# Two layers of attention and GLU on one core: a table of step orders for even and odd units, and the stages of the last tiles set apart

## The chip, the core and the metric

The kernel runs on one core of a Trainium2 chip. The core has TensorE (PE; its weight loads are listed apart as PEld), VectorE (DVE), ScalarE (ACT), GpSimd (POOL) and SyncE (SP), each with its own in-order instruction stream. SP issues nearly all transfers, POOL a few. The metric is device time in microseconds (us); lower is better.

## The reference

The input x is 2048 x 448. Attention, GLU, attention, GLU are applied with the same weights in both layers, each on a layer-normalised input and added to x. Attention has 16 heads of 28 for the queries, and one shared head of 28 for keys and values:

```python
q = (x @ wq).reshape(B, S, H, Dh).transpose(0, 2, 1, 3)
k = x @ wk
v = x @ wv
p = softmax(einsum("bhqd,bkd->bhqk", q, k) * Dh ** -0.5)
x = x + einsum("bhqk,bkd->bhqd", p, v)[heads side by side] @ wo
g, u = x_n @ w_gate, x_n @ w_up        # x_n: layer norm of x; 448 -> 1792
x = x + (sigmoid(g) * u) @ w_down
```

## The kernel before, in words

**Numbers.** Products run on pairs of half-precision tensors, a high and a low part. So a product of depth 448 is a chain of 11 matmuls (`chain`, L345), and the down product takes 3 matmuls for each of its 14 slices of 128 (L784).

**Units and steps.** Each layer has 16 units `u` of 128 queries, and each unit 16 steps `kt` of 128 keys, so 256 steps to a layer. A step has three kinds of attention work on PE:

- `S` (`scores`, L581): one matmul `s` (L584) for four heads; ACT takes its exponential into a tile `P` (L587). A step has four.
- `P` (`pv`, L590): the four matmuls `pv` (L595) of a finished step's `P` with the values. The trace shows each as two records, so one step is "x8" and two steps are "x16". These steps stand in a list `waiting`.
- `M` (a step of `Maxima`, L489): four matmuls `mx` (L549) into four PSUM banks and four DVE reductions `mp` (L554), for the row maxima of a later unit. A finished row of maxima is transposed (`mt`, L575), copied (`mr`, L577) and stored by POOL into row 28 of that unit's query tile `QS` (L578). Its place is set by a count of visits (`late`, L579).

`F` is a slice of filler (`Filler.slice`, L864): matmuls of any generator that has work, up to a budget of estimated ns. Fillers are the GLU of a block of two tiles (`bulk`, L732: `gp`, `up`, `dn`), the query projections `qp` (`qgen`, L425) and the output products `wo` (L685, three to a slice, ahead of the others). `X` is a tick (L610): each chain of stages in `side` counts down and runs its next stage when its count is zero. It also sets the budget of the following slices, from the filler that is left over the steps that are left. Operations put off by `defer` (L66) run a given number of slices later.

**Order.** PE takes its instructions in the order in which the program writes them. For the first units (u below 4 in layer 0, below 3 in layer 1) a string of letters gives one step (`ORDER`, `LATER`, L1037 and L1041); for all others `PAIR` (L1042) gives a step of even and a step of odd `kt`. In `PAIR` both `P` of a pair stand together in the even step.

**PSUM.** `s`, `mx` and every filler's accumulator share one tag `f` of seven banks; `pv` has the eighth.

**Stages of a tile** (`Block.tile`, L631). After a unit ends, 11 stages bring its rows to the block's input: the sums go out to memory and back (`f0` L639, `fx` L647), are inverted (`fy`), stored (`fz` L657), read back broadcast (`fw` L664, tile `lb`), multiplied on POOL (`fa` L669), split on ACT and DVE (`fb`, tile `oT`), then the products `wo` (`fc`), layer norm (`fd`), a transposing transfer on SP (`fe`, L340, tile XT2) and the start of the block's GLU (`ff`). The number before each stage is the ticks that it waits.

**Keys of the next layer** (L788 to L843). After a tile's `dn` its layer norm (`db`), transpose (`dc` by a transfer on SP, or `dct` on PE for the last block), product `kv` (`dd`), the transpose of the keys (`de`, `det`) and the count (`df`) follow, again by ticks.

**The tails.** After step 255 of a layer a loop (L1121) ticks and fills until the next layer's first unit has its maxima, or, in layer 1, until nothing is left. The list `fine` becomes non-empty when the last tile's `dn` is done, and the loop then uses other slices.

**Query tiles.** `load_qs` (L438) brings the next unit's `QS` (two buffers) by 12 transfers on SP (L445).

## Time and profile before

| what | us |
|---|---|
| three runs: median (lowest to highest) | 2290.93 (2286.94 to 2293.14) |
| the profiled execution: its own time | 2284.06 |
| its span, first to last instruction | 2282.3 |
| PE busy | 2213.4 (97%) |
| DVE busy | 1638.6 (72%) |
| ACT busy | 1545.7 (68%) |
| POOL busy | 338.1 (15%) |

The profiled execution is 6.9 us below the median of the three runs. A row of the timeline reads: start, duration, engine, line, operation, what it writes and reads, sizes, count; in brackets the idle time of the engine before it, and what ended that. [...]

### The profile page before, as it was taken

What the parts mean: (1) busy time and instruction counts of PE and PEld (TensorE: products, weight loads), DVE (VectorE), ACT (ScalarE), POOL (GpSimd) and SP (SyncE); (2) the same over time, 40 slices, a digit from 0 to 9 for tenths busy, and PEclk for the clock granted to TensorE, in tenths of its full rate; (3) what the DMA queues carried; (4) which work ended last, traced back from release to release, by engine and by line L of the source; (5) the groups of instructions that cost most, each with busy time, mean ns of one, the idle gap of its engine ahead of it and who ended that gap; (6) DMA issues with size and microseconds to landing.
All of it is one profiled execution on the core that took longest, in us unless ns stands there. A gap on an engine that the chain in (4) does not pass through costs nothing.

```text
span 2282.3 us, 41511 instructions
## 1 busy us (share of the span) xinstructions
PE 2213.4 (97%) x15915; PEld 1030.0 (45%) x15915; DVE 1638.6 (72%) x2905; ACT 1545.7 (68%) x2595; POOL 338.1 (15%) x590
## 2 busy tenths in 40 slices
PE   8998999999999999999999999999999999999989
PEld 3322353444545444454563224444444545444456
DVE  7988887777777777777795547777777777777322
ACT  5797786666667677676514997767676767667731
POOL 5114781001110110001011111000000000000010
PEclk9999999999999999999999999999999999999999
DMA  4333661323313142332341123233232313232233
GB/s 144 101 109 97 206 220 45 107 71 97 113 51 113 41 121 65 97 104 75 107 134 39 31 60 103 73 90 94 84 88 65 99 42 116 63 92 86 77 108 111
DMA packets 203623, 213.29 MB, mean 93 GB/s; under 512 B 135376, under 2 KB 164240, under 8 KB 203424
## 3 DMA queue, kind: packets, MB, share of 16 engines
q1 hardware_dynamic: 198080, 195.78, 29.5%
q0 software_dynamic: 5344, 14.87, 1.8%
q8 instruction: 124, 2.03, 0.4%
q14 instruction: 75, 0.61, 0.1%
HBM read 175.37 MB, written 23.59 MB: 87 GB/s over the span
## 4 chain that ended last, share of the span: by engine, by line
PE 59%; DVE 6%; ACT 3%; DMA 1%; issue 1%; SPq 0%; POOL 0%; ACTq 0%; DVEq 0%; POOLq 0%
PE pv L595 14%; PE s L584 13%; PE dn L784 9%; PE up L352 8%; PE gp L352 7%; PE mx L549 4%; DVE mp L554 4%; PE wo L695 2%; ACT P L587 2%; PE qp L352 1%; ACT h L757 0%; DVE th L754 0%; DMA rc<-sums 0%; DVE h L758 0%; DMA XT<-hl 0%
## 5 line engine op out<-in xcount | busy, mean ns | idle before, releaser
L587 ACT ACTIVATE P<-s,esc 128x512 f32<-128x512 f32 x2048 | 1291.4, 689 | 477.1 <-PE s L584 462.1
L554 DVE TENSOR_REDUCE mp<-mx 128x1 f32<-128x512 f32 x2048 | 1269.1, 682 | 398.6 <-PE mx L549 395.7
L584 PE MATMUL s<-QS,KK 96*128 96x512 f16 x2048 | 699.3, 380 | 29.7 <-DVE mp L554 12.0
L352 PEld LDWEIGHTS <-wgu 128*128 128x128 f16 x4928 | 456.3, 97 | 231.3 <-issue 89.8
L595 PE MATMUL pv<-P,VV 128*32 128x512 f32 x4096 | 506.0, 602 | 0.6 <-ACT pvs L599 0.6
L352 PE MATMUL gp<-XT,wgu 128*128 128x256 f16 x2464 | 364.7, 273 | 0.7 <-ACT P L587 0.6
L352 PE MATMUL up<-XT,wgu 128*128 128x256 f16 x2464 | 362.4, 273 | 0.8 <-DVE mp L554 0.4
L784 PE MATMUL dn<-WD,h 128*128 128x448 f16 x1344 | 314.4, 353 | 0.0
L584 PEld LDWEIGHTS <-KK 96*128 96x128 f16 x2048 | 198.1, 98 | 142.6 <-issue 44.3
L595 PEld LDWEIGHTS pv<-P,VV 128*32 128x32 f32 x4096 | 101.3, 109 | 263.6 <-issue 259.9
L549 PE MATMUL mx<-KK,QH 32*128 32x512 f16 x1792 | 188.4, 385 | 3.3 <-DVE mp L554 2.2
L784 PEld LDWEIGHTS <-h 128*128 128x128 f16 x1344 | 122.3, 97 | 139.4 <-issue 30.6
L549 PEld LDWEIGHTS <-QH 32*128 32x128 f16 x1792 | 46.1, 91 | 256.3 <-issue 253.2
L669 POOL TENSOR_TENSOR lb<-pvs,lb 128x512 f32<-128x512 f32 x32 | 40.9, 1278 | 627.3 <-DMA lb<-sums 446.1
L757 ACT ACTIVATE h<-th 128x512 f16<-128x512 f32 x112 | 70.5, 630 | 88.5 <-DVE th L754 88.5
L352 PE MATMUL qp<-XT,WQ 128*128 128x512 f16 x352 | 115.4, 387 | 1.0 <-DVE mp L554 0.4
L306 POOL TENSOR_SCALAR rs<-mv 128x1 f32<-128x1 f32 (+1 forms) x50 | 12.1, 242 | 693.5 <-DVE mv L291 647.7
L746 ACT ACTIVATE th<-gp,gsc 128x512 f32<-128x512 f32 x112 | 77.1, 688 | 40.7 <-PE gp L352 40.4
L754 DVE SCALAR_TENSOR_TENSOR th<-th,up 128x512 f32<-128x512 f32 x112 | 75.8, 677 | 35.3 <-PE up L352 34.7
L695 PE MATMUL wo<-WO,oT 128*128 128x448 f16 x384 | 94.5, 358 | 6.5 <-ACT oT L675 6.1
L758 DVE SCALAR_TENSOR_TENSOR h<-th,h 128x512 f16<-128x512 f32 x112 | 77.9, 696 | 31.3 <-ACT h L757 30.7
L352 PEld LDWEIGHTS <-WQ 128*128 128x128 f16 x352 | 33.2, 98 | 62.5 <-issue 37.7
(151 smaller groups left out, 915.9 us busy)
## 6 DMA issues: line engine op xcount, KB each, us to landing
wgu<-wgu_d SPq DMA_DIRECT2D x224, 512.0 KB
QS<-qd SPq DMA_DIRECT2D x384, 32.0 KB
lb<-sums SPq DMA_DIRECT2D x128, 64.0 KB
xr<-in_A_x_dram SPq DMA_DIRECT2D x32, 224.0 KB
qd<-qst POOLq DMA_DIRECT2D x28, 256.0 KB, 2.7
wgu_d<-sgu POOLq DMA_DIRECT2D x14, 512.0 KB, 4.2
x2d<-x SPq DMA_DIRECT2D x16, 224.0 KB
xr<-x2d SPq DMA_DIRECT2D x16, 224.0 KB
```

Of the source, the lines that this page charges most:

```text
L352: nc.tensor.matmul(ps, a, b, start=n == 0, stop=n == 10)
L549: nc.tensor.matmul(ps[h][:, i * w:(i + 1) * w], qh[32 * h:32 * h + 32, g], KK[l][32 * h:32 * h + 32, 1, ka:kz], start=True, stop=True, til ...
L554: nc.vector.tensor_reduce(o, ps[h].rearrange("p (g k) -> p g k", g=n), axis=AX.X, op=OP.max)
L584: nc.tensor.matmul(s, KK[l][0:96, 0, kt * 128:(kt + 1) * 128], QS[l, u][:, g].rearrange("p h n -> p (h n)"), start=True, stop=True)
L587: nc.scalar.activation(p, s, AF.Exp, scale=esc)
L595: nc.tensor.matmul(v[32 * g:32 * g + 32], VV[l][:, kt], P[g], start=kt == 0, stop=kt == KT - 1, tile_position=(0, 32 * g))
L695: nc.tensor.matmul(p, v["oT"][:, a, h * 128:(h + 1) * 128], WO[:, c, h], start=n == 0, stop=n == 11)
L746: defer(lambda: nc.scalar.activation(th, gp.rearrange("p j n -> p (j n)"), AF.Tanh, scale=gsc))
L754: nc.vector.scalar_tensor_tensor(t, th, 1.0, up.rearrange("p j n -> p (j n)"), op0=OP.add, op1=OP.mult)
L757: nc.scalar.activation(h[:, 0], t, AF.Copy, scale=2.0 ** -17)
L758: defer(lambda: nc.vector.scalar_tensor_tensor(h[:, 1], t, 2.0 ** -17, h[:, 0], op0=OP.mult, op1=OP.subtract), 1)
L784: nc.tensor.matmul(p, hs[f // 2][:, a, o:o + 128], WD[:, f, c], start=n == 0, stop=n == 3 * FC - 1)
```

## The change

Six things change; the numbers of instructions on PE stay the same.

1. `PATHS` holds a pair of orders for each stretch: A for the first four units of layer 0 (as before), B0 and B1 for its later even and odd units, C for the first three units of layer 1, D0 and D1 for its later even and odd units. Where both steps of a pair have a `P`, each `P` does all that waits, else one step.
2. The next unit's `QS` is loaded at `kt` 9 and no longer at 5. In D1 the odd step holds two `M`, so that the load, which stands in the branch of `M`, is written twice there. The second goes to the same buffer.
3. In the tails a tick has three slices of 600 and no longer four of 450. Once `fine` holds the last tile, a tick has four slices of 450 and no longer two.
4. The keys' stages: the transfer `dc` one tick after `db`, `kv` four ticks later; `dct` and `det` of the last block's first tile one tick later each.
5. GLU: the split of `h` on ACT three slices after `th` (two before), its low part on DVE two slices later (one before).
6. Layer 1's units 0 to 2: `fd` one tick later. `Maxima` of the next layer is made two steps later, a row of maxima for units 1 to 3 is stored one visit earlier, and layer 1 starts with half a query product of filler (three quarters before).

```diff
-        late.append([2 if l and u in AHEAD else LT, fin, (l, u)])
+        late.append([1 if l and u in AHEAD else LT, fin, (l, u)])
...
-            return ..., (3 + (l and u < 3), fd), (3, fe), (2, ff)
+            return ..., (3 + 2 * (l and u < 3), fd), (3, fe), (2, ff)
...
-                                                                     op1=OP.subtract), 1)
-                    defer(parts, 2)
+                                                                     op1=OP.subtract), 2)
+                    defer(parts, 3)
...
-                    later((2, db), (2, dct), (1, dd), (1, det), (1, df))
+                    later((2, db), (3, dct), (1, dd), (2, det), (1, df))
                 else:
-                    later((2, db), (3, dc), (2, dd), (2, de), (2, df))
+                    later((2, db), (1, dc), (4, dd), (2, de), (1, df))
...
-    ORDER = "FSFSFSFSPXM"
-    LATER = "FSFSFSPFSXM"
-    PAIR = ("FSFSXFSSPPM", "FSSFSXFSFM")
-    HEAD = U * KT - 32
+    HEAD = U * KT - 30
+    PATHS = {
+        "A": ("FSFSFSFSPXM", "FSFSFSFSPXM"),
+        "B0": ("SFSFSXSPPM", "SSXFFSFFSMF"),
+        "B1": ("FFSSXFFSSPMP", "SSFSFXSFM"),
+        "C": ("FXFFSSSSPPM", "SFFFSSSFXMFF"),
+        "D0": ("FSFSFXFSSPPM", "SSFFXSFSFM"),
+        "D1": ("FSFSXFSSPP", "MSFSSFXFFSM"),
+    }
...
-        fill.slice((0.75 if l else 0.4) * QCH)
+        fill.slice((0.50 if l else 0.4) * QCH)
...
-                    if kt == 5 and u + 1 < U:
+                    if kt == 9 and u + 1 < U:
                         load_qs(l, u + 1)
...
-                    for _ in range(len(waiting) if not paired else min(1, len(waiting))):
+                    for _ in range(len(waiting) if single else min(1, len(waiting))):
                         pv(*waiting.pop(0))
...
-            for _ in range(0 if fine else 4):
-                fill.slice(VS / 4)
+            for _ in range(0 if fine else 3):
+                fill.slice(VS / 3)
...
-            for _ in range(2 if fine else 0):
+            for _ in range(4 if fine else 0):
                 fill.slice(VS / 4)
```

How the instructions move is shown at three places.

**SP, the end of layer 1**: the stages of the last tile (`rc` is fx, `sums` fz, `lb` fw, the transpose into XT fe) among the loads of GLU weights (`wgu`) and the stores of the result. Before:

```order
L639 DMA sums_107<-pvs 4x512
L641 DMA xr<-x2d 128x448
L647 DMA rc<-sums_107 128x16
L657 DMA sums_107<-rc 128x16
L730 DMA wgu<-wgu_d 128x2048 x2
L664 DMA lb<-sums_107 32x512 x4
L730 DMA wgu<-wgu_d 128x2048 x2
L340 DMA_TRANSPOSE XT_28238<-hl 128x7x128
L796 DMA out_dram<-x_28506 128x448
```

With the change:

```order
L639 DMA sums_107<-pvs 4x512
L641 DMA xr<-x2d 128x448
L647 DMA rc<-sums_107 128x16
L730 DMA wgu<-wgu_d 128x2048 x2
L657 DMA sums_107<-rc 128x16
L664 DMA lb<-sums_107 32x512 x4
L730 DMA wgu<-wgu_d 128x2048 x2
L796 DMA out_dram<-x_28583 128x448
L340 DMA_TRANSPOSE XT_28316<-hl 128x7x128
```

A pair of weight loads has moved ahead of the store of the inverted sums, and a store of the result ahead of the transposing transfer. On PE, at the same place, the 12 `wo` matmuls have moved. Counting from the last `pv`, before there stand `gp` x7, `up` x22, `gp` x22, `up` x14, then `wo` x12, then `up` x8, `gp` x22, `up` x22 and `dn` x84. With the change there stand `gp` x7, `up` x22, `gp` x22, `up` x22, `gp` x22, `up` x22 and `dn` x8 ahead of `wo`, and `dn` x76 behind it.

**PE, the boundary between the layers**, from the transpose of the last tile (L335) on: `kv` and the keys' transposes (L388, L389), the last maxima, their transpose, and the first score of layer 1 (L584). "..." stands for the same row again. Before:

```order
L335 MATMUL t_16045<-id_79,hl 128x128
...
L352 MATMUL kv<-WKV,XT_15026 128x56
...
L352 MATMUL qp<-XT_8465,WQ 128x512
...
L388 MATMUL kvt<-id_79,ktl_112 128x128
...
L352 MATMUL qp<-XT_8465,WQ 128x512
...
L549 MATMUL mx<-KK,QHB 128x128
...
L352 MATMUL qp<-XT_8465,WQ 128x512
...
L575 MATMUL mt<-id_79,m_16137 16x128
```

With the change:

```order
L335 MATMUL t_16078<-id_79,hl 128x128
...
L352 MATMUL kv<-WKV,XT_15026 128x56
...
L388 MATMUL kvt<-id_79,ktl_112 128x128
...
L549 MATMUL mx<-KK,QHB 128x128
...
L575 MATMUL mt<-id_79,m_16165 16x128
```

The query products `qp` that stood between these steps (2, 4 and 15) now stand ahead of the last transpose. Between the last `dn` and that transpose there are now 40 `qp` and both the transpose and the keys of the tile before; before there were 21 `qp` and those keys. Behind `mt` there are 7 `qp` (8 before) until the first `s`.

**PE, layer 0, the first steps of an odd unit** (unit 9; `gp` belongs to the next block). Before:

```order
L784 MATMUL dn<-WD,h 128x448
...
L584 MATMUL s<-QS,KK 128x512
...
L595 MATMUL pv<-P,VV 32x512 x8
L549 MATMUL mx<-KK,QH 128x512
...
L784 MATMUL dn<-WD,h 128x448
...
L352 MATMUL gp<-XT_7793,wgu 128x256
```

With the change:

```order
L784 MATMUL dn<-WD,h 128x448
...
L584 MATMUL s<-QS,KK 128x512
...
L595 MATMUL pv<-P,VV 32x512 x4
L549 MATMUL mx<-KK,QH 128x512
...
L595 MATMUL pv<-P,VV 32x512 x4
L584 MATMUL s<-QS,KK 128x512
...
L352 MATMUL gp<-XT_7799,wgu 128x256
```

The two steps of `pv` now have the maxima between them, and the filler of the old block ends before the unit's first score: eight scores, two `pv` and one `mx` group follow one another without filler in units 7 to 15, some four such steps in unit 5. In layer 1's first three units the other thing happens: 48 single blocks of `pv` become 24 double ones.

More of the change, by code (lines that the diff above doesn't have):

```diff
@@ L724, in tile @@
             slow = 2 if l == 0 and u < 4 else 1
-            return (1, f0), (1, fx), (slow, fy), (1, fz), (1, fw), (slow, fa), (slow, fb), (2, fc), (3 + (l and u < 3), fd), (3, fe), (2, ff)
+            return (1, f0), (1, fx), (slow, fy), (1, fz), (1, fw), (slow, fa), (slow, fb), (2, fc), (3 + 2 * (l and u < 3), fd), (3, fe), (2, ff)
         def load_w(self, f):
@@ L1036, in interleaved_layers_kernel, with pair_of @@
     early[0] = False
-    ORDER = "FSFSFSFSPXM"
     MORE = (10,)
-    HEAD = U * KT - 32
+    HEAD = U * KT - 30
     sparse = ()
-    LATER = "FSFSFSPFSXM"
-    PAIR = ("FSFSXFSSPPM", "FSSFSXFSFM")
+    PATHS = {
[6 more added lines that the diff above has]
+    }
+    def pair_of(l, u):
+        if not l and u < 4:
+            return PATHS["A"]
+        if l and u < 3:
+            return PATHS["C"]
+        return PATHS["BD"[l] + str(u % 2)]
     FIRST = KT * TB + 17
@@ L1072, in interleaved_layers_kernel @@
             P = []
-            paired = (l or u > 3) and u > 2
-            if paired:
-                order = PAIR[kt % 2]
-            else:
-                order = LATER if l and step < 3 * KT and step - 1 in sparse else ORDER
-            for o in order:
+            pair = pair_of(l, u)
+            single = "P" in pair[0] and "P" in pair[1]
+            for o in pair[kt % 2]:
                 if o == "S":
@@ L1112, in interleaved_layers_kernel @@
                 else:
-                    fill.slice(2 * rate / (PAIR[0] + PAIR[1]).count("F") if paired else rate / ORDER.count("F"))
+                    fill.slice(2 * rate / "".join(pair).count("F"))
             waiting.append((l, u, kt, P))
```

## The prediction

> **What bounds the kernel now.** I read the page first, then the busy times by stage, then the timeline of PE where a stage has idle time.
>
> ```profile
> PE 2213.4 (97%) x15915; PEld 1030.0 (45%) x15915; DVE 1638.6 (72%) x2905; ACT 1545.7 (68%) x2595; POOL 338.1 (15%) x590
> L587 ACT ACTIVATE P<-s,esc 128x512 f32<-128x512 f32 x2048 | 1291.4, 689 | 477.1 <-PE s L584 462.1
> L554 DVE TENSOR_REDUCE mp<-mx 128x1 f32<-128x512 f32 x2048 | 1269.1, 682 | 398.6 <-PE mx L549 395.7
> ```
>
> PE is the bound: ACT and DVE wait for it, 462.1 and 395.7 us. The change keeps every PE instruction. So it can move the time in two ways only: through PE's idle time, and through what PE loses between unlike matmuls. The stages, in order (us of the window, then busy time of PE, PEld, DVE, ACT, POOL with counts, the granted clock, the DMA's share and GB/s):
>
> ```profile
> 0.00:317.00 317.00, 286.64 (x1925) 102.98 (x1926) 272.56 (x533) 245.10 (x450) 138.78 (x170) 0.98 0.46 143
> 317.00:1115.00 798.00, 784.22 (x5746) 370.96 (x5744) 602.98 (x1062) 554.13 (x919) 102.13 (x215) 1.00 0.31 88
> 1115.00:1234.00 119.00, 113.78 (x912) 70.46 (x905) 95.18 (x171) 27.40 (x51) 17.30 (x38) 1.00 0.36 108
> 1234.00:1366.00 132.00, 127.35 (x758) 34.91 (x756) 67.22 (x118) 120.27 (x203) 15.26 (x29) 1.00 0.15 41
> 1366.00:2187.00 821.00, 816.50 (x5963) 390.67 (x5962) 580.40 (x991) 583.34 (x950) 60.67 (x131) 1.00 0.29 84
> 2187.00:2282.30 95.30, 84.86 (x627) 60.07 (x624) 20.24 (x32) 15.48 (x25) 4.00 (x9) 0.96 0.36 112
> ```
>
> These are layer 0's first four units (order A, unchanged), its later units (B), its tail, layer 1's first three units (C), its later units (D), and the last tail. PE idles 30.4, 13.8, 5.2, 4.7, 4.5 and 10.4 us in them. Only the last five are touched: 38.6 us in all. The last tail has most idle time for its length, and a clock below 1.
>
> **The last tail: -7.3 us.** Its timeline shows one wait:
>
> ```profile
> 2190.14 2.56 PE L352 MATMUL up<-XT,wgu 128*128 128x256 f16 x22
> 2192.54 2.56 PE L352 MATMUL gp<-XT,wgu 128*128 128x256 f16 x22
> 2194.57 0.85 SPq L730 DMA_DIRECT2D wgu<-wgu_d  x2
> 2195.56 1.74 SPq L664 DMA_DIRECT2D lb<-sums  x4
> 2200.80 1.26 POOL L669 TENSOR_TENSOR lb<-pvs,lb 128x512 f32<-128x512 f32 x1 [27.73 <-DMA lb<-sums]
> 2202.75 0.69 DVE L676 TENSOR_TENSOR oT<-lb,oT 128x512 f16<-128x512 f32 x1 [6.69 <-ACT oT L675]
> 2202.77 4.15 PE L695 MATMUL wo<-WO,oT 128*128 128x448 f16 x12 [6.14 <-ACT oT L675]
> 2206.76 1.04 PE L352 MATMUL up<-XT,wgu 128*128 128x256 f16 x8
> 2212.44 16.05 PE L784 MATMUL dn<-WD,h 128*128 128x448 f16 x84
> 2212.85 1.25 SPq L340 DMA_TRANSPOSE XT<-hl  x1
> 2203.00:2207.00 4.00, 4.00 (x15) 1.62 (x14) 0.48 (x2) 0.31 (x1) 0.00 (x0) 0.59 0.02 4
> ```
>
> PE runs out of filler and waits 6.14 us for `oT`, whose low part is ready at 2203.44. Then the clock is 0.59, and the 12 `wo` take 2206.76 - 2202.77 = 3.99 us. At 16.05 / 84 = 0.19 us each they would take 2.29. So the stall costs 6.14 + 1.70 = 7.8 us.
>
> With the change five groups of 22 at 2.40 us (2192.54 - 2190.14) and 8 `dn` stand between the seven `gp` and `wo`: PE arrives at 2190.14 + 12.0 + 1.5 = 2203.7, after `oT`. The filler is moved, not added, so the whole stall is won if the chain of stages stays as early. It may not: the pair of weight loads that stood between fz and fw now stands ahead of fz. The nearest row is `lb`: issued behind such a pair until 2197.3, it is multiplied only at 2200.8. If fz instead of fw lies behind the pair, I reckon up to 1 us later for `oT`, half of it on the path: 7.8 - 0.5 = 7.3. Behind `wo` the layer norm and the transposing transfer of the tile must be covered; before its transfer was issued 2212.85 - 2206.76 = 6.1 us after `wo`, and the 76 `dn` cover 14.5 us, also with the transfer behind the store of a result (34 `dn`, 6.5 us after `wo`). Bounds: -7.8, and -1.8 if the wait comes back whole as 6 us.
>
> **The boundary of the layers: +2.1 us.** Here a chain sets the end, not PE's work:
>
> ```profile
> 1214.74 1.67 PE L352 MATMUL qp<-XT,WQ 128*128 128x512 f16 x7
> 1216.25 0.45 PE L352 MATMUL kv<-WKV,XT 128*128 128x56 f16 x11
> 1221.07 0.55 PE L335 MATMUL t<-id,hl 128*128 128x128 f16 x7
> 1225.70 0.40 PE L549 MATMUL mx<-KK,QHB 32*128 32x128 f16 x16
> 1229.57 0.22 PE L575 MATMUL mt<-id,m 128*16 128x128 f16 x1
> 1230.89 0.73 POOL L421 DMA_DIRECT2D qd<-qst  x1 [1.41 <-issue]
> 1231.63 0.53 POOL L578 DMA_DIRECT2D QS<-mr  x1
> 1233.66 0.61 PE L584 MATMUL s<-QS,KK 96*128 96x512 f16 x2 [2.03 <-DMA QS<-mr]
> 1230.00:1234.00 4.00, 1.97 (x10) 0.75 (x9) 0.04 (x1) 0.62 (x2) 2.79 (x4) 1.00 0.20 69
> ```
>
> From the last `dn` (1214.74) to the last transpose (1221.07) go 6.33 us, from there to the first score 12.59: keys, their transpose, maxima, their transpose, the store. With the change 40 `qp` stand ahead of that transpose, at (1216.25 - 1214.74) / 7 = 0.216 us each 8.6, with 0.9 for the earlier tile's transpose, keys and their transposes: 9.5 us, 3.2 later. Behind it the chain is the same, but POOL no longer stores `qp` in front of the maxima's row, since all 44 `qp` are done: 1231.63 would be about 1230.3, so -1.3. The earlier tile's transpose (0.49) was paid ahead of 1214.74 and counts off; 51 `qp` instead of 54 are done, 0.65 left for later. 3.2 - 1.3 - 0.5 + 0.65 = 2.1. Bounds: 0 (the chain was the limit anyway) and +5.2, once more PE's whole idle time of this stage.
>
> [...] Row first: behind the wait of 6.14 us the clock was 0.59, in the window of the wait of 2.03 us before 1233.66 it stayed at 1.00. [...]
>
> **Layer 1's first units: -5.4 us.** One `pv` block against two in one:
>
> ```profile
> 1502.79 1.92 PE L595 MATMUL pv<-P,VV 128*32 128x512 f32 x16
> 1504.64 0.39 PE L549 MATMUL mx<-KK,QH 32*128 32x512 f16 x4
> 1236.99 0.38 PE L584 MATMUL s<-QS,KK 96*128 96x512 f16 x1
> 1237.30 1.06 PE L595 MATMUL pv<-P,VV 128*32 128x512 f32 x8
> 1238.30 0.60 PE L584 MATMUL s<-QS,KK 96*128 96x512 f16 x2
> ```
>
> A single block takes 1238.30 - 1237.30 = 1.00 us, a double one 1504.64 - 1502.79 = 1.85; entering from `s` costs 1237.30 - 1236.99 - 0.22 = 0.09. One join saves 2.00 + 0.09 - 1.85 = 0.24; I take 0.225, since rows round to 0.01. 24 joins: -5.4. Whether it shows depends on ACT, busy 120.27 of 132 us here: the floor is -11.7, above what PE can give. Other end: 0, if ACT sets the pace.
>
> **Layer 0's later units: +2 us.** In the odd units each pair is parted again by `mx`. The entry is not paid twice (`mx` to `pv` costs what `mx` costs to anything), so each parting costs 2.00 - 1.85, say 0.14: 6 units x 8 pairs = 48, +6.7. Against that:
>
> ```profile
> 400.98 0.10 PEld L352 LDWEIGHTS <-XT 128*128 128x128 f16 x1 [1.60 <-DMA XT<-hl]
> 403.13 0.67 PE L352 MATMUL kv<-WKV,XT 128*128 128x56 f16 x11 [3.23 <-ACT P L587]
> 394.40 0.38 PE L584 MATMUL s<-QS,KK 96*128 96x512 f16 x1 [0.20 <-DVE mp L554]
> 403.00:407.00 4.00, 3.87 (x26) 1.42 (x29) 2.70 (x6) 2.80 (x7) 0.00 (x0) 0.50 1.00 337
> 662.00:728.00 66.00, 64.22 (x500) 31.52 (x497) 50.42 (x91) 46.46 (x80) 6.19 (x16) 1.00 0.39 106
> 728.00:793.00 65.00, 64.99 (x461) 29.62 (x459) 48.83 (x85) 44.98 (x74) 6.17 (x16) 1.00 0.22 63
> ```
>
> The first `kv` waits 3.23 us for its transposed tile (the weight load's row names the transfer), and 1.3 more go at clock 0.50. With `dc` issued two ticks earlier that transfer has two steps more: -4.5. Odd units (66.00 - 64.22 = 1.8 us idle) lose more than even ones (0.01); B1 spaces the two `M` of a pair more evenly, and I take a fifth of 10 us: -2. The filler-free start of six odd units adds waits on banks such as the 0.20 at 394.40; one or two each, +1.8. 6.7 - 4.5 - 2 + 1.8 = 2.0. Bounds: -7 (all 13.8 idle us won) and +19 (below).
>
> **Layer 1's later units: 0.** PE idles 4.5 us in 821: that is all a better order can win. Going by the nearest row, layer 0's 13.8 of 798, a worse one costs 821 x 0.0173 - 4.5 = 9.7. D has as many joins and `M` as before; between the ends I take no change.
>
> **At nothing:** `QS` at `kt` 9 still has 7 steps of some 4 us ahead of its unit. The second load of the odd units (six times 12 issues) lands in the same buffer, and SP is then free until the next weights are released. GLU's later parts are covered by the next GLU chain of 4.8 us, `fd` by a stage's slack; without that cover each costs one slice, 0.6 us, per tile.
>
> **The sum.** -7.3 + 2.1 - 5.4 + 2.0 + 0 = -8.6 us on the profiled execution's 2284.06 (span 2282.3 and 1.8 around it). The median of the runs shown is 6.9 us above that execution, so I take the same difference from it: 2290.93 - 8.6 = **2282.3**.
>
> **Rivals.**
>
> 1. *The last wait stays* (the change doesn't do there what it says): `oT` comes as late after PE's arrival as before, since fz now queues behind 1 MB of weights. For it: `lb` behind such a pair took 3.5 us from its last issue. Against it: the pair starts earlier too, at 2192.6. -8.6 + 6 = -2.6: 2288.3, no change.
> 2. *ACT sets the pace of layer 1's first units*, and joined blocks become idle PE. For: 91% busy. Against: 11.7 us are free. -3.2: 2287.7, no change.
> 3. *Layer 0's odd units stall at their start* (slower): eight scores without filler meet exponentials of 0.69 us and reductions of 0.68 on seven banks, and the unit's first `pv` or `kv` waits. For: the only long wait of this stage, 3.23 us, lies in such a stretch. Against: it was a transfer's, and the banks' waits there were 0.20. At 3.23 for six units, +19.4: 2301.7. From 2.6 us each, (8.6 + 6.9) / 6, the result is slower.
> 4. *C and D fill the idle time*: C to ACT's floor (-6.3 more), D 3 us: 2273.
>
> **How the numbers follow.** What this kernel's measurement can tell from no change is about 0.3%, 6.9 us: faster is below 2284.1, slower above 2297.8. Forecast 0.45, its own range 2277 to 2288; it lies only 1.8 us below the bound, so 0.33 of it counts as faster and 0.12 as same. Rivals 1 and 2: 0.15 each, same. Rival 3: 0.12, slower. Rival 4: 0.13, faster. Faster 0.46, same 0.42, slower 0.12. The range takes in rivals 1, 2 and 4 and leaves out rival 3 and the ends beyond rival 4: 2271 to 2294.
>
> **What would show it.** In the last tail: no wait before `wo`, a clock of 1.00, PE's idle time down from 10.4 to about 3 us. At the boundary: `t` to the first `s` in some 11.3 us, with waits before `kvt`, `mx` and `mt`, and the stage 2 us longer. In the first three units of layer 1: 132 us become about 127. In layer 0's odd units: no wait of 3 us before `kv`, no wait over 1 us at their first scores. A wait before `wo` above 2 us, or idle time of PE above 20 us between units 4 and 15 of layer 0, would make the forecast wrong.

## The result, and the profile after

The changed kernel takes **2264.75 us** (median, 2261.7 to 2268.98), the kernel before 2291.95 in the same comparison: ratio 0.9887, 95% interval 0.9864 to 0.9909. It is faster by 1.1%, about three times the 8.6 us forecast, and lies below the range of 2271 to 2294. In five later comparisons the kernel before had medians of 2288.0 to 2289.8, and 2288.6 over their runs together, so the gain is nearer to 24 us than to 27. One run of fine_alone below (7526.9 us) and one of the kernel before beside it (3076.68) were slow ones and are left out of the medians.

First the page of the changed kernel, then its busy times by stage (us of the window, then PE, PEld, DVE, ACT, POOL with counts, the clock, the DMA's share, GB/s). The stages are those of the prediction, but cut at the first score of a unit and at the last `pv`, so that unit 15 of layer 0 stands with the boundary.

```profile
PE 2209.2 (98%) x15915; PEld 1032.6 (46%) x15915; DVE 1639.5 (72%) x2905; ACT 1558.1 (69%) x2595; POOL 337.7 (15%) x590
```

```profile
0.00:318.40 318.40, 288.61 (x1919) 103.51 (x1919) 271.61 (x531) 243.70 (x449) 138.53 (x170) 0.97 0.46 142
318.40:1053.40 735.00, 729.12 (x5308) 341.08 (x5305) 560.82 (x984) 512.79 (x846) 96.61 (x201) 1.00 0.30 87
1053.40:1229.46 176.06, 170.24 (x1350) 97.90 (x1348) 140.14 (x250) 70.00 (x125) 23.17 (x53) 0.98 0.36 111
1229.46:1360.40 130.94, 124.91 (x753) 38.96 (x752) 67.21 (x118) 118.64 (x202) 14.25 (x27) 1.00 0.15 40
1360.40:2179.04 818.64, 815.68 (x5989) 392.04 (x5987) 579.40 (x991) 598.19 (x952) 61.10 (x131) 1.00 0.30 88
2179.04:2263.50 84.46, 80.62 (x609) 59.12 (x605) 20.33 (x32) 14.79 (x23) 3.99 (x9) 1.00 0.37 120
```

Cut in the same way, the kernel before stands beside it. The third column gives the other traces below in which that stage's code is the old one.

| stage | before, profiled execution | old code, other traces | changed | predicted |
|---|---|---|---|---|
| layer 0, units 0 to 3 | 316.8 | 316.1 to 319.5 | 318.4 | 0 |
| layer 0, units 4 to 14 | 738.3 | 737.7 to 738.8 | 735.0 | +2.0, with unit 15 |
| unit 15 and the boundary | 178.6 | 178.6 to 178.8 | 176.1 | +2.1 |
| layer 1, units 0 to 2 | 132.0 | 132.9 to 134.4 | 130.9 | -5.4 |
| layer 1, units 3 to 15 | 823.7 | 823.6 to 825.2 | 818.6 | 0 |
| from the last `pv` | 92.9 | 92.1 to 94.3 | 84.5 | -7.3 |

By the third column the changed stages gain 3.5, 2.6, about 3, 5 and 8.4 us: some 22 of the 24. The two profiled executions differ by less, 18.5 us (2284.06 and 2265.6): that of the kernel before is short in the first units of both layers (316.8 and 132.0 us), where other traces of the same code take up to 319.5 and 134.4 (see the last section).

The last tail, by its timeline, has no wait before `wo`:

```profile
2189.43 2.56 PE L352 MATMUL up<-XT,wgu 128*128 128x256 f16 x22
2190.88 1.27 POOL L669 TENSOR_TENSOR lb<-pvs,lb 128x512 f32<-128x512 f32 x1 [28.13 <-DMA lb<-sums]
2191.83 1.68 PE L784 MATMUL dn<-WD,h 128*128 128x448 f16 x8
2192.83 0.69 DVE L676 TENSOR_TENSOR oT<-lb,oT 128x512 f16<-128x512 f32 x1 [3.46 <-ACT oT L675]
2193.34 2.43 PE L695 MATMUL wo<-WO,oT 128*128 128x448 f16 x12
2195.61 4.70 PE L784 MATMUL dn<-WD,h 128*128 128x448 f16 x24
```

`oT`'s low part is ready at 2193.52, and the twelve `wo` take 2195.61 - 2193.34 = 2.27 us at a clock of 1.00. Their row lasts 2.43 us and reaches past the next start; here and below, what a group of matmuls takes is the distance between starts. At the boundary of the layers the waits stand where the change puts them:

```profile
1217.53 0.55 PE L335 MATMUL t<-id,hl 128*128 128x128 f16 x7
1221.90 0.23 PE L388 MATMUL kvt<-id,ktl 128*128 128x128 f16 x1 [1.61 <-DVE ktl L381]
1226.30 0.28 PE L575 MATMUL mt<-id,m 128*16 128x128 f16 x1 [3.04 <-DVE m L570]
1226.51 3.11 PE L352 MATMUL qp<-XT,WQ 128*128 128x512 f16 x7
1229.46 1.03 PE L584 MATMUL s<-QS,KK 96*128 96x512 f16 x4
```

Seven `qp` take 2.95 us to the first score, 0.42 each and twice the usual 0.216: behind the wait of 3.04 us the granted clock is 0.51 (from 1226.0 to 1229.5), and from the first score on it is 1.00. It fell ahead of that wait, which begins at 1223.26: the clock is 1.00 from 1222.0 to 1222.5, behind the wait of 1.61 us for `kvt`, and 0.50 from 1223.0 on.

### The profile page after: what moved, and what is told of

Read it like the earlier page. It is cut to its first block, busy times and chain, and to the rows that moved or that the text cites. A ratio compares the mean times of both kernels' runs of the same rounds, so it can differ in the third digit from the quotient of the medians.

```text
span 2263.5 us, 41590 instructions
## 1 busy us (share of the span) xinstructions
PE 2209.2 (98%) x15915; PEld 1032.6 (46%) x15915; DVE 1639.5 (72%) x2905; ACT 1558.1 (69%) x2595; POOL 337.7 (15%) x590
## 4 chain that ended last, share of the span: by engine, by line
PE 85%; DVE 7%; ACT 3%; issue 2%; DMA 1%; POOL 1%; SPq 1%; ACTq 0%; DVEq 0%; POOLq 0%
PE pv L595 20%; PE s L584 18%; PE gp L352 12%; PE up L352 12%; PE dn L784 11%; PE mx L549 7%; DVE mp L554 5%; PE wo L695 3%; ACT P L587 2%; PE qp L352 2%; DMA wgu_d<-sgu 0%; PE hot L916 0%; DMA rq<-in_A_wq_dram 0%; ACT qst L406 0%; POOL qst L414 0%
## 5 line engine op out<-in xcount | busy, mean ns | idle before, releaser
L587 ACT ACTIVATE P<-s,esc 128x512 f32<-128x512 f32 x2048 | 1307.2, 690 | 478.0 <-PE s L584 462.7
L554 DVE TENSOR_REDUCE mp<-mx 128x1 f32<-128x512 f32 (+1 forms) x2048 | 1268.5, 681 | 404.3 <-PE mx L549 401.0
L584 PE MATMUL s<-QS,KK 96*128 96x512 f16 x2048 | 684.0, 381 | 21.4 <-DVE mp L554 10.9
L352 PEld LDWEIGHTS <-wgu 128*128 128x128 f16 x4928 | 468.3, 97 | 183.0 <-issue 46.4
L352 PE MATMUL gp<-XT,wgu 128*128 128x256 f16 x2464 | 345.6, 272 | 2.0 <-DVE mp L554 0.7
L352 PE MATMUL up<-XT,wgu 128*128 128x256 f16 x2464 | 342.5, 272 | 0.6 <-DVE mp L554 0.2
L784 PE MATMUL dn<-WD,h 128*128 128x448 f16 x1344 | 299.6, 352 | 0.2 <-DVE mp L554 0.2
L584 PEld LDWEIGHTS <-KK 96*128 96x128 f16 x2048 | 187.0, 98 | 207.9 <-issue 122.8
L352 PE MATMUL qp<-XT,WQ 128*128 128x512 f16 x352 | 110.6, 391 | 0.6 <-POOL WQ L137 0.2
L695 PE MATMUL wo<-WO,oT 128*128 128x448 f16 x384 | 88.0, 352 | 1.6 <-DVE mp L554 1.4
```

What stands on the lines that cost most here:

```text
L352: nc.tensor.matmul(ps, a, b, start=n == 0, stop=n == 10)
L554: nc.vector.tensor_reduce(o, ps[h].rearrange("p (g k) -> p g k", g=n), axis=AX.X, op=OP.max)
L584: nc.tensor.matmul(s, KK[l][0:96, 0, kt * 128:(kt + 1) * 128], QS[l, u][:, g].rearrange("p h n -> p (h n)"), start=True, stop=True)
L587: nc.scalar.activation(p, s, AF.Exp, scale=esc)
L695: nc.tensor.matmul(p, v["oT"][:, a, h * 128:(h + 1) * 128], WO[:, c, h], start=n == 0, stop=n == 11)
L784: nc.tensor.matmul(p, hs[f // 2][:, a, o:o + 128], WD[:, f, c], start=n == 0, stop=n == 3 * FC - 1)
```

## The experiments

Times are ratios to the kernel before on the same chip, with the 95% interval; "of the changed kernel" compares medians with 2264.75. "Changed, ... as before" takes one part out of the changed kernel; "before, ..." puts one part into the kernel before. By ratios, against no_tail and qs_once, the costs of no_glu, no_part, no_keys and no_d come out 1 to 2 us smaller than by medians, and an interval reaches some 3 us to either side. So costs of 3 to 5 us rest on the stages of the traces more than on the times.

| run | edit | median us | ratio to before |
|---|---|---|---|
| tail_alone | before, three slices of 600 in the last tail | 2289.00 | 1.0004 (0.9996 to 1.0013) |
| no_tail | changed, four slices of 450 there | 2265.36 | 0.9893 (0.988 to 0.9907) |
| fine_alone | before, four slices where `fine` holds, last tail only | 2279.09 | 0.9954 (0.9941 to 0.9968) |
| b_alone | before, orders B | 2286.59 | 0.9984 (0.9975 to 0.9993) |
| keys_alone | before, keys' stages | 2291.15 | 1.0009 (1.0000 to 1.0018) |
| c_alone | before, orders C | 2285.39 | 0.9984 (0.9974 to 0.9994) |
| d_alone | before, orders D | 2287.59 | 0.9993 (0.9985 to 1.0002) |
| glu_alone | before, GLU's later parts | 2286.12 | 0.9986 (0.9976 to 0.9996) |
| bound_alone | before, boundary | 2289.95 | 1.0003 (0.9994 to 1.0012) |
| no_glu | changed, GLU's parts as before | 2275.37 | 0.9935 (0.9923 to 0.9947) |
| no_part | changed, `pv` of odd units joined | 2274.09 | 0.9926 (0.9914 to 0.9938) |
| no_keys | changed, keys' stages as before | 2269.97 | 0.9912 (0.9898 to 0.9925) |
| no_d | changed, old orders for D | 2269.98 | 0.9913 (0.9898 to 0.9928) |
| no_bound | changed, boundary as before, `QS` loaded once | 2268.02 | 0.9911 (0.9898 to 0.9925) |
| qs_once | changed, `QS` loaded once | 2264.16 | 0.9897 (0.988 to 0.9913) |
| lag33, lag42, mix | changed, other lags of the GLU | 2268.28, 2269.01, 2266.41 | 0.9906, 0.9911, 0.9906 |

### Which edit emptied the last tail

tail_alone, and no_tail with the sign turned:

```diff
-            for _ in range(0 if fine else 4):
-                fill.slice(VS / 4)
+            parts = 3 if final else 4
+            for _ in range(0 if fine else parts):
+                fill.slice(VS / parts)
```

> The kernel before, with one edit: four slices of filler per round in the last tail become three of 600 ns, so that the stages stand closer in slices to the work behind them (the last tail alone; the boundary of the layers keeps its four). Theory A (places): the gain of each part is what the two traces differ by at its place, so the last tail gives -8.4 us (92.9 to 84.5 from the last pv to the end) and the median goes from 2292 to about 2283.5. Theory B (clock): the part of the 27 us that the two profiled executions do not show (8.4) belongs to the clock, because the long wait before wo lowers it by a length that differs from run to run; then this edit alone gives -12 to -17 (2275 to 2280), and its runs show a mean clock nearer to 0.997 than the kernel before. No wait before wo in either.

> The changed kernel with the last tail alone as before (four slices of 450 ns per round). Theory A: the 6 us wait before wo is back and the time is 2264.75 + 8.4 = 2273. Theory B: 2277 to 2281, with a lower mean clock. If the later orders of layer 1 hold the filler otherwise, the wait may not come back: then the stage is as long as in the changed kernel and the slices were not what removed it.

Neither changed the time beyond its interval. A timeline of tail_alone still has the wait:

```profile
2204.76 4.66 PE L695 MATMUL wo<-WO,oT 128*128 128x448 f16 x12 [5.68 <-ACT oT L675]
```

The list `fine` gets its entry at the end of layer 0 and is never emptied, so layer 1's tail runs through the other loop from its first tick. There the filler per tick goes from two slices of 450 ns to four: the stages of the last tile stand twice as far apart in filler. fine_alone changes that number alone:

```diff
-            for _ in range(2 if fine else 0):
+            for _ in range((4 if final else 2) if fine else 0):
```

> The kernel before with one number changed, and that for layer 1's tail only: four slices of 450 ns behind each tick in place of two (the list fine is filled at the boundary of the layers and never emptied, so this loop, and not the one with the slices of 600, runs in the last tail). Theory A (places): the wait of 5.8 to 6.1 us before wo and the 1.7 to 2.0 at a low clock go, the last tail falls from 93 to 84.5, the median from 2289.0 to 2280.5. Theory B (clock): more than 12 us, 2277 or less, and the mean clock rises. Rival: the wait went because of layer 1's new orders, and the tail stays at 93: 2289.

```profile
2206.16 1.68 PE L784 MATMUL dn<-WD,h 128*128 128x448 f16 x8
2207.68 2.60 PE L695 MATMUL wo<-WO,oT 128*128 128x448 f16 x12
```

There is no wait before `wo`. The tail falls to 84.8 us and the time by 10.5 us (7.3 to 13.5), the medians by 9.1. Of the parts put in alone this is the largest gain. Theory B, that the clock makes it more than 12, is not needed: the stage itself gives 8.1 (92.9 to 84.8).

### Layer 0's later units: orders and keys

Where no diff is shown, the edit is that part of the change's own diff, put into the kernel before or taken out of the changed one.

> The kernel before with layer 0's new pair orders alone (units 4 to 15; the keys' stages as before). Theory A1: the partings of 48 pv pairs cost +8.1 in matmul time and the waits before kv stay, the waits before scores fall by 5 and those between maxima rise by 5: stage 4 to 14 about 8 us longer, median 2300. Rival A3: the orders space the maxima, so the waits on their banks before kv (7.5 us) go with them alone: stage 738 or shorter, median 2288 to 2292. The difference of the two is in the waits before kv in this stage: 7 us and 0.

> The kernel before with the three numbers of the keys' stages of layer 1 moved (the transposing transfer two rounds earlier, the keys four behind it, the end one behind): nothing else. Theory A1: this edit removes the waits before kv in units 4 to 14 of layer 0 (7.5 us in the trace of before), so this stage falls from 738.3 to about 731 and the median by 7. Rival A2: only the first kv wait, the one on the transfer (3.23 us and 1.3 at half clock), goes: -4.5. Rival A3: the waits are on the banks that the maxima hold, which the pair orders set; then the waits at kv stay and the time is the same within 2 us.

The rows of units 4 to 14 in the kernel before, in b_alone, and in no_part, which comes next:

```profile
316.80:1055.10 738.30, 725.66 (x5288) 342.25 (x5286) 556.77 (x981) 511.18 (x845) 96.55 (x200) 1.00 0.30 86
319.40:1056.20 736.80, 730.51 (x5308) 340.98 (x5305) 560.18 (x984) 512.52 (x846) 97.89 (x201) 1.00 0.33 87
318.60:1060.20 741.60, 728.78 (x5308) 345.44 (x5305) 560.11 (x984) 514.30 (x846) 96.19 (x201) 1.00 0.30 86
```

With the orders alone units 4 to 14 take 736.8 us: PE is busy 4.9 us longer than before (730.51 against 725.66) and idle 6.3 us less (6.3 against 12.6). No wait of more than 0.25 us before `kv` is left, though the keys' transfer stands where it was; the longest wait of the stage is 0.6 us. That is what rival A3 said of the orders, and A1's account of the keys falls. But the transfer has its part in the first wait: the keys' edit alone shortens the stage by 1.9 us (736.5; the first wait before `kv` falls from 3.23 to 1.69 us), as A2 in part had it, and lengthens the end of the layer by 4.4 (183.0), where a wait of 1.7 us and a stretch at a clock of 0.79 appear; it is no gain by itself. Then the parting itself:

```diff
-        "B1": ("FFSSXFFSSPMP", "SSFSFXSFM"),
+        "B1": ("FFSSXFFSSPPM", "SSFSFXSFM"),
```

> The changed kernel with the two pv of layer 0's odd units joined again (order FFSSXFFSSPPM; the maxima behind both). The prediction's price of a parting, 0.14 us, gives 48 x 0.14 = 6.7 us less matmul time: 2258.5, if the waits stay. Rival: the parting is what spaces the maxima; joined, the waits on their banks come back (7.5 us before kv in the kernel before, 1.7 without them): 2263 to 2267. They are told apart by the matmul time and the waits of units 4 to 14 (706.2 and 28.8 us in the changed kernel).

Joining costs 9.3 us, more than even the rival's 2267. In its trace units 4 to 14 take 741.6 us, and PE idles 12.8 us where the changed kernel idles 5.9. By the distances between starts the `pv` of these units take 5.6 us less (162.5 after 168.1), 0.14 for each of 40 partings, as reckoned (in the changed kernel `mx` to `pv` takes 0.33 us, 688.82 to 689.15, and `mx` to `gp` 0.33, 684.67 to 685.00); so the lost spacing costs some 12 us. PE's busy time falls by only 0.3 us, since a short wait lengthens a row instead of showing as idle time (the four `mx` at 695.81 below take 0.87 us and not 0.40). Among the waits that do show, those of scores for DVE's reductions rise from 1.3 to 3.5 us. The timelines of unit 9 show why. Joined:

```profile
685.66 0.39 PE L549 MATMUL mx<-KK,QH 32*128 32x512 f16 x4
688.27 0.46 PE L549 MATMUL mx<-KK,QH 32*128 32x512 f16 x4
693.35 0.40 PE L549 MATMUL mx<-KK,QH 32*128 32x512 f16 x4
695.81 0.87 PE L549 MATMUL mx<-KK,QH 32*128 32x512 f16 x4
698.14 0.38 PE L584 MATMUL s<-QS,KK 96*128 96x512 f16 x1 [0.26 <-DVE mp L554]
686.08 5.10 DVE L554 TENSOR_REDUCE mp<-mx 128x1 f32<-128x512 f32 x8 [1.16 <-PE mx L549]
```

Parted, the changed kernel:

```profile
681.06 0.40 PE L549 MATMUL mx<-KK,QH 32*128 32x512 f16 x4
684.67 0.40 PE L549 MATMUL mx<-KK,QH 32*128 32x512 f16 x4
688.82 0.40 PE L549 MATMUL mx<-KK,QH 32*128 32x512 f16 x4
692.28 0.56 PE L549 MATMUL mx<-KK,QH 32*128 32x512 f16 x4
681.48 2.48 DVE L554 TENSOR_REDUCE mp<-mx 128x1 f32<-128x512 f32 x4 [0.30 <-PE mx L549]
```

The four reductions of a group keep DVE for 2.48 us. Joined, the groups follow at 2.6, 5.1 and 2.5 us, and DVE runs eight reductions on end for 5.10 us while their banks stay taken; parted, they follow at 3.6, 4.2 and 3.5. One block of `pv`, 1.0 us, has moved from the wide gap into the narrow one.

> The changed kernel with the keys' stages of layer 1 as before. Alone this edit took 1.9 us off units 4 to 14 of layer 0 (738.5 to 736.5) and made the end of the layer 4.4 us longer (178.6 to 183.0), while with all edits that end is 2.6 us shorter. Theory A (places add up): units 4 to 14 at 736.8 as with the orders alone, the end at 176: 2267. Rival: the longer end is this edit's whatever the order, and another edit hides it; then taking it back gives an end of 172 and 2262.

Without the keys' edit the changed kernel is 5.2 us slower: units 4 to 14 take 737.5 us (737 by theory A; one wait before `kv` is back, 0.68 us), but the end of the layer 178.0, not 176. So the same three numbers cost 4.4 us there before the new orders and save 2 behind them; what turned the sign there was not separated further.

### GLU's later parts and the orders D

> The kernel before with the orders D for layer 1's later units alone. The prediction said 0 (between -4.5 and +9.7). Theory A: the waits of scores behind up and gp on their bank (7.0 us together in the trace of before) go: stage 823.7 to 818.7, median 2284. Rival: they go because of the later parts of the GLU (three and two slices in place of two and one), and D alone leaves the stage at 822 to 825.

> The changed kernel with the GLU's later parts as before (two slices and one, in place of three and two). The prediction put this edit at nothing. Theory G: the orders D alone took 1.5 us off layer 1's later units, all edits together took 5, and the rest is this edit's, since the tile h then does not stand between scores and their banks: units 3 to 15 of layer 1 from 818.7 to 822, the median from 2265 to 2268.5. Rival: the rest comes from the query tiles' load at the tenth step or from other edits: 818.7 and 2265.

```diff
-                                                                     op1=OP.subtract), 2)
-                    defer(parts, 3)
+                                                                     op1=OP.subtract), 1)
+                    defer(parts, 2)
```

The edit that the prediction put at nothing is worth 10.6 us in its place, three times what theory G gave it: 4.1 in units 4 to 14 (739.1), 1.0 in the end of the layer, 5.4 in layer 1's later units (824.0). The groups of operations say where (busy us, mean ns, idle time before them). Without it:

```profile
L757 ACT ACTIVATE h<-th 128x512 f16<-128x512 f32 x112 | 70.3, 628 | 87.4 <-DVE th L754 87.2
L758 DVE SCALAR_TENSOR_TENSOR h<-th,h 128x512 f16<-128x512 f32 x112 | 81.2, 725 | 38.4 <-ACT h L757 38.4
```

With it:

```profile
L757 ACT ACTIVATE h<-th 128x512 f16<-128x512 f32 x112 | 70.1, 626 | 63.8 <-DVE th L754 63.8
L758 DVE SCALAR_TENSOR_TENSOR h<-th,h 128x512 f16<-128x512 f32 x112 | 76.4, 683 | 28.1 <-ACT h L757 28.1
```

Two things differ: ACT and DVE wait for each other less (23.6 and 10.3 us), and DVE's low half of `h` is shorter by 42 ns in the mean. The wait, in the timeline of no_glu, late in layer 1:

```profile
1960.86 0.68 DVE L754 SCALAR_TENSOR_TENSOR th<-th,up 128x512 f32<-128x512 f32 x1
1961.37 0.40 PE L549 MATMUL mx<-KK,QH 32*128 32x512 f16 x4
1961.57 0.63 ACT L757 ACTIVATE h<-th 128x512 f16<-128x512 f32 x1 [0.44 <-DVE th L754]
1962.23 0.69 DVE L758 SCALAR_TENSOR_TENSOR h<-th,h 128x512 f16<-128x512 f32 x1 [0.70 <-ACT h L757]
1962.84 1.88 DVE L554 TENSOR_REDUCE mp<-mx 128x1 f32<-128x512 f32 x3
1963.58 0.82 PE L352 MATMUL up<-XT,wgu 128*128 128x256 f16 x6 [0.38 <-DVE mp L554]
```

and the same place of the changed kernel:

```profile
1953.52 0.68 DVE L754 SCALAR_TENSOR_TENSOR th<-th,up 128x512 f32<-128x512 f32 x1
1954.03 0.46 PE L549 MATMUL mx<-KK,QH 32*128 32x512 f16 x4
1954.45 2.48 DVE L554 TENSOR_REDUCE mp<-mx 128x1 f32<-128x512 f32 x4 [0.26 <-PE mx L549]
1956.86 0.68 DVE L758 SCALAR_TENSOR_TENSOR h<-th,h 128x512 f16<-128x512 f32 x1
```

With the short lag, `h`'s low half stands ahead of the reductions in DVE's queue; DVE idles 0.70 us for ACT and then works 0.69 on `h`, while the banks of `mx`, begun at 1961.37, wait, and PE with them. With the long one the reductions go first, and `h` runs when ACT's half has long been there. The shorter operation is the second part, told in the last section. PE's waits that stand right behind an `h` for which DVE had idled, and that end with a reduction, come to 5.3 us in units 4 to 14 and layer 1's later units of no_glu: 2.0 behind an `h` of usual length and 3.3 behind a lengthened one. The changed kernel has none of them. So both parts count; the other half of the 10.6 us does not show as waits of PE and was not traced further.

> The kernel before with the GLU's later parts alone (three slices and two in place of two and one). Theory G1 (the edit by itself: DVE no longer stands waiting for ACT's half of h with the maxima's reductions behind it): layer 1's units 3 to 15 from 823.8 to 818.5, layer 0's units 4 to 14 from 738.5 to 734.5, the median from 2288.6 to 2279. Theory G2 (the lags suit the new orders only, since slices lie otherwise in the old ones): less than 3 us in all, 2286 or more, and DVE's idle time before h's low part stays near 31 us.

> The changed kernel with layer 1's later units in the old pair order, the GLU's later parts kept. Theory G1: the orders D are worth what they gave alone, 1.5 us: units 3 to 15 at 820, the median 2266.5. Theory G2: the lags lose their effect there, the stage is back at 823.5 and the median at 2269.5.

D alone is within its interval of no change, as d_alone's rival had it. Neither G1 nor G2 held as put: the lags alone take 2.4 us off layer 1's later units (821.3), D alone 1.1 (822.6), both 5.1. In layer 0 the lags alone win 0.5 us, not 4. Without D the changed kernel has 822.0 there and is 5.2 us slower. The idle time before `h` does fall with the lags alone (31.3 to 26.2 us), and no wait for DVE's reductions right behind an `h` of usual length is left. But eight of its operations now meet POOL (726 ns in the mean), and in layer 0 the waits of `kv` for transposed tiles grow from 0.6 to 2.9 us, which takes back about what the banks give there. With the new orders no wait before `kv` is left in units 4 to 14.

The lags of ACT's half and of DVE's are (3, 3) in lag33, (4, 2) in lag42, and in mix (4, 2) in layer 0 and (3, 2) in layer 1; all three load `QS` once.

> The changed kernel with the query tile loaded once and h's low part on DVE one slice later still (three slices, then three). By the place in DVE's queue: DVE's idle time before h's low part (28.1 us) falls further, by some 5 to 15 us, and if PE's waits follow as they did in the first step (10 us for 10.3), 2258 to 2261. Rival: the waits that are left lie where nothing waits for DVE: 2264, the same.

> The changed kernel with the odd units' query tile loaded once (no difference by itself: 2264.2) and ACT's half of h one slice later still (four slices, then two). If what counts is that the four reductions stand ahead of h's low part in DVE's queue, the waits are the same and the time too (2263 to 2266). If the waits behind th on ACT (63.8 us before h in the changed kernel) are what delays the scores' exponentials, another 2 to 4 us go: 2260 to 2262. Against it: h's low part may now fall among the reductions of the next group, +3.

> The changed kernel with the query tile loaded once and ACT's half of h four slices late in layer 0 and three in layer 1. Stage by stage from the run with four in both: layer 0's units 4 to 14 at 733.8 in place of 735.1, the end of the layer at 175.5, layer 1 as in the changed kernel (818.7): 1.7 us less, 2262.5 against 2264.2. Rival: other stages shift by as much, and it is the same within 1 us.

None of the other lags is a gain. In lag33 the idle time before `h` falls by 5.4 us and no stage gets shorter: what is left there holds nobody up. lag42 has 733.8 in layer 0's later units but 820.5 in layer 1's; mix, which keeps it out of layer 1, showed 736.8 there in its one trace, at a clock of 0.96 to 0.97 in its first 100 us, so the 1.2 us are not confirmed. By their ratios the three lie 2 to 3 us above qs_once, within the intervals; their profiled executions are 4 to 5 us longer than its own in layer 0's first units alone (319.4 to 320.5 against 315.3), whose order none of the edits touches.

### The other parts

> The kernel before with the orders C for layer 1's first three units alone. The prediction said -5.4. Theory A: the 24 joins take 4.6 us off the matmuls and come back as waits (scores on ACT's exponentials, maxima on DVE): the stage goes from 132.1-134.4 to 130.9-132.9, -1.5, the median to 2287.5. Rival: these waits came from the later fd and the smaller head of filler, not from C; then C alone gives -4 to -5, 2284.5, with no more than 7 us of waits between scores and between maxima together.

C alone is worth 3.7 us (1.4 to 5.9), between the two theories. Its stage takes 130.1 us, against 132.0 in the kernel before, both at a clock of 1.00 around their start (1225 to 1245 and 1215 to 1250); by the distances between starts the blocks of `pv` take 4.1 us less (42.5 after 46.6), and the scores and maxima together 2.6 more (65.4 after 62.8). Waits of scores for DVE's reductions rise from 1.0 to 2.6 us, those of maxima for ACT's exponentials from 0.2 to 1.3. So more than half of the joins' gain went into waits.

> The kernel before with the boundary's edits alone (three slices of 600 per tick, later the last block's first keys, four slices once the last tile is done, half a query product at layer 1's start; layer 1's tail as before). The prediction said +2.1 for this. Theory A: in the changed kernel that stage is 2.6 us shorter, but with another order in front of it; alone it gives between -3 and +1: 2286 to 2290, with the waits before kvt and mt of 1.6 and 3.0 us and half the clock behind them for 6.8 us. Rival: the shorter stage comes from unit 15's order, and the boundary's edits cost the predicted 2 us: 2291.

> The changed kernel with the boundary's edits taken back (stages of the last block's first keys, slices until the last tile is done, two slices after it, three quarters of a query product), the last tail's four slices kept and the odd units' query tile loaded once. Prediction's term: they cost 2.1, so 2262 without them. As they did alone: they cost 1.1 in the stage from unit 15 to the first score (179.7 against 178.6): 2263, with that stage at 175. Rival: in front of the new orders they are what makes this stage 176.0: 178 to 179 without them, 2267.

Alone, the boundary's edits make their stage 1.1 us longer and the time the same within its interval; in the changed kernel taking them back costs 3.3 us (the stage 177.4, layer 1's first units 132.7), which is the rival's side. Since b_alone had 176.4 there with the old boundary, the 2.6 us of this stage come first from unit 15's order. Why the same edits lose alone and win behind the new orders was not traced.

```diff
-                    if kt == 9 and u + 1 < U:
+                    if kt == 9 and u + 1 < U and (l, u + 1) not in QS:
```

> The changed kernel with the odd units' query tile of layer 1 loaded once and not twice (72 transfers fewer on SP). The prediction put the second load at nothing: the same within 1 us (2264.3 to 2266.3), the same stage of 818.7. Rival: SP's queue and the memory are held up by it, and the stage gets 1 to 3 us shorter.

The second load of the query tile costs nothing that can be measured, as predicted. Four small edits had no run of their own: the load at `kt` 9, the later `fd`, the later `Maxima` and the earlier store of its rows.

## Why the prediction was wrong

**The last tail (-7.3)** was right in mechanism and size: -8.4 in the stage, no wait, clock 1.00, PE idle 3.8 us. fz's place behind the weights did not bring the wait back, and rival 1 falls.

**The boundary (+2.1)**: the waits came where expected, and from the last transpose to the first score it took 11.9 us (11.3 expected), though the seven `qp` in it, at a clock of 0.51, took 2.95 us and not 1.51, for which the sum has no term. From the last `dn` to the last transpose it took 9.4 us (9.5 expected, 6.3 before). So this chain was right. What the sum missed lies ahead of the last `dn`, where it took 0.5 us off: from unit 15's first score to there it takes 154.7 us instead of 159.6, 157.3 with the orders B alone and 158.5 with the boundary's edits alone. The stage is 2.5 us shorter and not 2.1 longer.

**Layer 1's first units (-5.4)**: the matmul price was near (4.1 measured in `pv` alone), but more than half came back as waits, which is rival 2 in part; ACT's exponentials are one cause of these, DVE's reductions the other. The stage is 130.9 and not 127.

**Layer 0's later units (+2.0)** is the first step that failed. "B1 spaces the two `M` of a pair more evenly, and I take a fifth of 10 us": the spacing was the main thing. PE's idle time in units 4 to 14 fell from 12.6 to 5.9 us. The partings cost what was reckoned (5.6 us for 40 of the 48), and yet joining them again costs 6.6 us of the stage, so there the spacing is worth some 12 us and not 2. "The first `kv` waits 3.23 us for its transposed tile" was read as the transfer's alone. Moving the transfer takes 1.5 us off it, and the orders remove all of it. Rival 3 falls: no first score of an odd unit waits over 0.4 us.

**"At nothing: GLU's later parts"** is the second, and the larger. The step asked only what cover hides a later `h` and what it costs without it; it did not ask what stands behind `h` in DVE's queue, though the idle times before `h` on ACT and DVE stood on the page of the kernel before, and the cost to PE in its timeline:

```profile
L757 ACT ACTIVATE h<-th 128x512 f16<-128x512 f32 x112 | 70.5, 630 | 88.5 <-DVE th L754 88.5
L758 DVE SCALAR_TENSOR_TENSOR h<-th,h 128x512 f16<-128x512 f32 x112 | 77.9, 696 | 31.3 <-ACT h L757 30.7
1579.18 0.69 DVE L758 SCALAR_TENSOR_TENSOR h<-th,h 128x512 f16<-128x512 f32 x1 [0.70 <-ACT h L757]
1580.53 0.38 PE L584 MATMUL s<-QS,KK 96*128 96x512 f16 x1 [0.37 <-DVE mp L554]
```

Taken back in the changed kernel, it costs 10.6 us. **"Layer 1's later units: 0"** fell with it: 5 us, of which D alone gives 1.1. Rival 4's time (2273) came nearest, by luck: its orders C did not fill ACT, its 3 us for D were 1.1, and the gains that were there it did not name.

**The carry to the median**: adding 6.9 us put the base at 2290.93; over the later runs the kernel before lies at 2288.6, 4.5 above that execution. The profiled executions differ by 18.5 us, so the sum missed 9.9 of the 17.6 us between 2282.3 and 2264.75. The other 7.7 lie between executions and medians: 2.3 because the base was too high, 4.5 because the profiled execution of the kernel before was short, and 0.9 because that of the changed kernel (2265.6) was above its median.

## What to carry to other kernels

An operation that waits on another engine should be costed by what stands behind it in its own queue: here putting it later was worth as much as the parting of `pv` (10.6 and 9.3 us when taken back), though only some 3 us without the new orders. Where a group of work needs a fixed time on a second engine (here 2.48 us of reductions), the even spacing of the groups can be worth more than the switches that it costs (here some 12 us against 5.6). Edits of an order do not add up: the keys' stages, the boundary and the GLU's lags, worth +2.1, +0.7 and -3 us alone, were worth some -5, -3 and -10 in their place, so a part should be judged by taking it out of the whole as well as by adding it.

## What the runs showed of the hardware

**DVE and POOL in each other's way.** In no_glu:

```profile
2025.79 0.63 ACT L757 ACTIVATE h<-th 128x512 f16<-128x512 f32 x1
2026.37 1.26 POOL L669 TENSOR_TENSOR lb<-pvs,lb 128x512 f32<-128x512 f32 x1 [25.64 <-DMA lb<-sums]
2026.45 1.73 DVE L758 SCALAR_TENSOR_TENSOR h<-th,h 128x512 f16<-128x512 f32 x1 [0.43 <-ACT h L757]
2028.84 0.38 PE L584 MATMUL s<-QS,KK 96*128 96x512 f16 x1 [0.96 <-DVE mp L554]
```

DVE's low half of `h`, 0.68 us elsewhere, takes 1.73 when POOL's multiplication of `lb` has begun 0.08 us earlier: until POOL ends at 2027.63, and 0.55 more. PE then waits 0.96 us for a bank. Others show the same sum: one in glu_alone takes 1.64 us at 823.00, until POOL ends at 824.09, and 0.55 more; in the kernel before those at 326.88, 348.38 and 1133.12 take 0.94, 0.94 and 1.53 and end 0.55, 0.55 and 0.53 us after the POOL operation that had begun ahead of them. Of the 112 such operations 6 took over 0.9 us in no_glu, 8 in glu_alone, 3 in the kernel before, none in the changed kernel. In the changed kernel one `h` begins first, at 476.20, 0.11 us ahead of POOL's multiplication: it takes 0.68 us, and the multiplication 1.69 in place of 1.26. The reductions show no such lengthening: the four at 1958.46 in no_glu, beside a multiplication from 1958.43 on, take 2.48 us as elsewhere; their mean is 681 to 683 ns in these traces, and the longest takes 694 in the kernel before and 693 in the changed one.

**The same wait, two clocks.** The kernel before and glu_alone both wait 2.03 us for `QS` before layer 1's first score. Window around it, before:

```profile
1215.00:1250.00 35.00, 29.46 (x205) 10.37 (x204) 17.43 (x35) 21.63 (x41) 9.74 (x12) 1.00 0.18 57
```

glu_alone:

```profile
1215.00:1250.00 35.00, 29.61 (x196) 10.81 (x198) 16.38 (x34) 18.89 (x36) 9.73 (x12) 0.90 0.16 49
```

From that score on the clock is 0.58 for 4.4 us and then 0.69 for 5 us in glu_alone (together the 0.90 of its window), and 1.00 in the kernel before, from 1233.66 to 1243; layer 1's first units take 134.3 and 132.0 us. The first units of layer 0, also in the same order, take from 315.3 to 320.5 us over all traces, with clocks of 0.93 to 0.98 in the first 100 us of the four traces read there; that the clock makes the whole difference is not shown. So the length of a wait alone does not tell what follows: behind 2.03 us the clock fell in one trace and stayed at 1.00 in the other. What decides it is not shown. In these two stages the profiled execution of the kernel before was up to 5 us shorter than other traces, which is about what it lies below the median. So a difference of two executions under some 5 us says little here without its stages.
